# Linear attention into a four-expert mixture on one core: a sixth sum buffer, token differences in 1 KB tiles, a shared rest buffer, and batch 1's q and x rests turned by DMA

## The chip, the cores and the metric

One core of a Trainium2 chip runs the whole kernel in one launch. The metric is device time in microseconds (us), from the launch to the end of the program on that core.

## The reference, cut to what matters

```python
def phi(x): return np.where(x > 0, x, np.exp(x) - 1.0) + 1.0
q_p, k_p = phi(q), phi(k)                          # q, k, v: 8 batches, 8 heads, 576 rows, 64 columns
kv  = np.einsum('bhsd,bhse->bhde', k_p, v)
z   = np.sum(k_p, axis=2)
num = np.einsum('bhsd,bhde->bhse', q_p, kv)
den = np.einsum('bhsd,bhd->bhs', q_p, z)[..., None] + 1e-06
x   = (num / den).transpose(0, 2, 1, 3).reshape(4608, 512)
p   = domain_probs / (domain_probs.sum(-1, keepdims=True) + 1e-09)
out = sum(p[:, e:e+1] * (np.maximum(x @ w1[e], 0) @ w2[e]) for e in range(4))
```

The first half makes 4608 tokens of 512 numbers out of eight batches of 576 rows; the second half sends every token through four two-layer networks (512 to 1024 to 512) and adds their outputs, weighted.

## The kernel before

**Tiles and batches.** A batch has 576 rows: 512 of them make one tile of 512 tokens, and the last 64 are its *rest*. The eight rests together make a ninth tile. The tiles run in the order 0 to 6, then the tile of the rests (8), then 7. While TensorE runs the two layers of one tile, the attention of a later batch is made beside it: batch b's x must stand, turned (columns on partitions), before tile b begins.

**A tile's two layers.** For each expert, `Block` (L883) makes the hidden rows in two halves d with seven products each, p1 to p7, a fast scheme for a 2 by 2 block product. It needs sums of the weights (`weight_sums`, `weight_sums2`) and four differences of the tile's turned x, which `token_sum` (L870) makes, on GpSimd from tile 1 on: `tt[0]` to `tt[3]`, each 128 x 2 x 256 in float16, 1 KB a partition. p5 reads `tt[0]`, p6 `tt[1]`, p7 `tt[2]`, p4 `tt[3]`. Layer 2 (`layer2_product`, L815) works the same way with sums of the hidden rows that GpSimd makes (`hidden_sum`, L800, tiles `hs`). `add_acc` (L728) weighs a product and adds it into one of four sums `acc` per tile (128 x 512, float32, 2 KB a partition): ScalarE writes a sum's half first (L734), VectorE adds to it (L736), and `store` (L714) sends the finished sum out from SyncE's DMA queue.

**A batch's attention.** SyncE's queue loads q, k and v in four pieces each (`load`, L325). `phi_act` and `phi_dve` (L357, L374) make phi on ScalarE and VectorE, `kv` (L464) the 64 x 65 products, `dma_qT` (L417) turns q with a DMA that transposes, `nd` and `norm` (L495, L485) make x, `dma_xT` (L551) turns x. The rests go the same way in small: `load_left` (L311) loads k, v and q rest into the tile `rl`; `left_act`, `left_v` and `left_dve` (L386 to L407) make phi; `dma_qTl` (L425) turns q rest into `qz` with two transposing DMAs; `nd_left` (L514) makes x rest `x_sl` and turns it into `xT_left` with two transposing DMAs. Batch 1 is the exception: `pe_qTl` (L433) and `pe_xl` (L442) turn its two rests on TensorE, two 128 x 128 transposes each, and ScalarE copies each result out of PSUM in two pieces.

**Buffers.** A pool keeps a number of equal buffers under a tag; a new tile takes one whose last reader has gone, and its first writer waits for that reader. The tags of interest: `acc` (5 buffers of 2 KB, NACC, L173), `tt` (2 of 4 KB, one for a tile's four differences; batch 0's x lies in one of them at first), `h` (5 of 4 KB, NHB, the hidden rows and batch 0's q), `rl` of batches 1 to 7 (one buffer of 3 KB with k, v and q rest side by side).

**What sets the order.** Nothing is reordered by a planner at build time. Each engine does its instructions in the order in which the program emits them. `CFG["EARLY"]` (L103) is a hand-written list of steps that is emitted first; it reaches to the beginning of tile 2. Everything behind it is emitted by positions: `batch_steps` (L963) and the loops below L1084 give each step a place (a tile has 56 units), and the steps are sorted by it. In the names of steps, `b2.q1` is batch 2's second piece of q, `b2.next` the loads of the next batch's rests, `ts2.3` the fourth difference of tile 2, `p5.131` product 5 of tile 1, expert 3, half 1, and `m12.60` a layer 2 product of tile 1, expert 2.

Of the kernel before, what the change touches and what calls it, by code (L numbers as in the profile page):

```python
# [11 lines left out]
FP32 = mybir.dt.float32  # L12
# [123 lines left out]
    ),  # L136
# [4 lines left out]
def kernel(  # L141
# [30 lines left out]
    DE = D + 1  # L172
    NACC = 5  # L173
    NHB = 5
# [122 lines left out]
    class Batch:  # L297
# [7 lines left out]
        def alloc_left(self):  # L305
            if self.b:
                self.rl = praw.tile([P, 3, HG, D], FP32, tag="rawl", bufs=1, name="rl")
            else:
                self.rl = pm.tile([P, 2, HG, D], FP32, tag="acc", bufs=NACC, name="rl")

        def load_left(self, *names, eng=nc.sync, us=(0, 1)):  # L311
            b = self.b
            if self.rl is None:
                self.alloc_left()
            for i, (name, src) in enumerate((("k", k), ("v", v), ("q", q))):
                for u in us:
                    if name in names:
                        eng.dma_start(
                            out=self.rl[u * HP : (u + 1) * HP, i if self.b else 0],
                            in_=src[b, u * HG : (u + 1) * HG, SM:S].rearrange(  # L320
                                "h r d -> r h d"
                            ),
                        )
# [62 lines left out]
        def left_act(self, *names):  # L386

            for name in names:
                i = ("k", "v", "q").index(name)
                src = self.rl[:, i if self.b else 0].rearrange("p h d -> p (h d)")  # L390
                parts = []
                for u in range(2) if name == "k" else ():
                    us = slice(u * HP, (u + 1) * HP)
                    parts.append((us, self.kl[us, 2 * u : 2 * u + 2].rearrange("p a d -> p (a d)")))
                if name == "q":
                    self.ql = pa.tile([P, HG, D], FP16, tag="qlp", bufs=1, name="qlp")
                    parts.append((slice(0, P), self.ql.rearrange("p h d -> p (h d)")))
                for us, dst in parts:
                    nc.scalar.activation(dst, src[us], AF.Identity, bias=1.0)
                el = aps([P, HG * D], FP32, "psum_el")  # L400
                nc.scalar.activation(el, src, AF.Exp)
                self.ph["l" + name] = el, parts
# [22 lines left out]
        def dma_qTl(self):  # L425
            for u in range(2):
# [4 lines left out]
                )  # L431

        def pe_qTl(self):  # L433
            ps = aps([P, 2, P], FP16, "psum_ql")
            for a in range(2):
                nc.tensor.transpose(out=ps[:, a], in_=self.ql[:, 2 * a : 2 * a + 2], identity=identh)
            yield
            for u in range(2):
                us = slice(u * HP, (u + 1) * HP)
                nc.scalar.copy(out=self.qTl[:, :, u, us], in_=ps[:, :, us])  # L440

        def pe_xl(self):  # L442
            ps = aps([P, 2, P], FP16, "psum_xl")
            for a in range(2):
                nc.tensor.transpose(out=ps[:, a], in_=self.xl[:, a], identity=identh)
            yield
            c0 = self.b * SL
            for u in range(2):
                us = slice(u * HP, (u + 1) * HP)
                nc.scalar.copy(out=xT_left[:, 2 * u : 2 * u + 2, c0 : c0 + SL], in_=ps[:, :, us])  # L450

# [62 lines left out]
        def nd_left(self, side_by_side=False):  # L514
# [15 lines left out]
            yield  # L530
            for u in range(2) if self.b != 1 else ():
                us = slice(u * HP, (u + 1) * HP)
                c0 = self.b * SL
                nc.sync.dma_start_transpose(
                    out=xT_left[:, 2 * u : 2 * u + 2, c0 : c0 + SL],
                    in_=self.xl[us].rearrange("p a i -> p (a i)"),
                )
# [22 lines left out]
    class First(Batch):  # L560

        def open(self):
            self.qp = pm.tile([P, CM, H, D], FP16, tag="h", bufs=NHB, name="qp")
            self.qT = pa.tile([P, CM, NPAIR, P], FP16, tag="qT", bufs=1, name="qT")
            self.x = pm.tile([P, NPAIR, CM, P], FP16, tag="tt", bufs=2, name="x_sb")
            self.new_xT()
# [303 lines left out]
    def token_sum(j, i, eng=nc.gpsimd):  # L870
        x = xT_of(j)
        if j not in tts:
            tts[j] = pm.tile([P, 4, 2, NH], FP16, tag="tt", bufs=2, name="tt")
        t = tts[j]
        b11, b12 = x[:, 0:2, 0:NH], x[:, 0:2, NH:NT]
        b21, b22 = x[:, 2:4, 0:NH], x[:, 2:4, NH:NT]
        a, b = ((b12, b11), (b22, t[:, 0]), (b22, b12), (b21, t[:, 1]))[i]
        eng.tensor_tensor(out=t[:, i], in0=a, in1=b, op=AO.subtract)  # L878

# [3 lines left out]
    class Block:  # L883
# [48 lines left out]
        def p6(self):  # L932
            self.products(self.b, lambda k: s_block(self.e, 1, k), tts[self.j][:, 1])
            yield
            self.u2 = self.copy("u2", 2)

        def p5(self):
            self.products(self.e5, lambda k: s_block(self.e, 0, k), tts[self.j][:, 0], True)

        def p7(self):  # L940
            self.products(self.b, lambda k: a_block(self.e, 1, 0, k), tts[self.j][:, 2])
            yield
# [5 lines left out]
        def p4(self):  # L948
            self.products(self.b, lambda k: a_block(self.e, 1, 1, k), tts[self.j][:, 3])
            yield  # L950
# [12 lines left out]
    def batch_steps(bt, nxt, put, at, at_next):  # L963
# [36 lines left out]
        put(at["kv"], f"b{b}.kv", bt.kv)  # L1000
        put(at["lqd"] + 1, f"b{b}.next", load_left, "k", "v")
        put(at["lqd"] + 1.001, f"b{b}.nextq", load_left, "q")
        if not first:
            put(at["lqd"] + 2, f"b{b}.qTl", bt.dma_qTl)
        if first:
            put(at["qtl"], f"b{b}.qTl", bt.pe_qTl)
            for i in range(NPAIR):
# [13 lines left out]
        else:  # L1021
            put(2 * NSLOT * E + at_next["kv"] - 1e-6, f"b{b}.nl", bt.nd_left, True)
        if first:
            put(at["xl"], f"b{b}.xl", bt.pe_xl)

# [158 lines left out]
```

## Time and profile before

| | |
|---|---|
| time, median of 3 runs | 483.46 us (482.79 to 484.04) |
| time of the profiled execution | 483.89 us |
| its span, first to last instruction | 482.1 us |
| granted TensorE clock, mean | 0.999 |
| TensorE matmul busy | 476.2 us, 99% of the span |
| VectorE, ScalarE, GpSimd busy | 379.1, 329.9, 358.8 us |
| DMA | 54.06 MB, 112 GB/s mean |

The profiled execution's time is 1.8 us longer than its span: that much lies before the first and behind the last instruction. In the profile's rows, PE is TensorE, PEld its weight load, DVE VectorE, ACT ScalarE, POOL GpSimd, SP SyncE; a q behind a name (SPq) is that engine's queue, which issues DMAs and waits. A timeline row reads: start, duration, engine, line, operation, what it writes and reads, count, and in brackets the idle time before it with what ended it.

### The profile page before, as it was taken

The numbers are of one execution on the slowest core, as the hardware profiler recorded it, in microseconds if no ns is written. First come the engines' busy times: TensorE is split into PE (matmuls) and PEld (weight loads), VectorE is DVE, ScalarE is ACT, GpSimd is POOL, SyncE is SP. The second block draws the span as 40 slices with busy tenths as digits, with TensorE's granted clock in tenths as the row PEclk, the third lists the DMA queues.
The fourth block names the chain that finished last, engine by engine and source line by source line (L and its number), as shares of the span: only waits on it lengthen the run. The fifth ranks groups of instructions, "written<-read, shape, count | busy, mean of one in ns | idle before, by whom it ended". The sixth has DMA issues, their size and how long they took to land.

```text
span 482.1 us, 12029 instructions
## 1 busy us (share of the span) xinstructions
PE 476.2 (99%) x4565; PEld 406.7 (84%) x4565; DVE 379.1 (79%) x794; ACT 329.9 (68%) x659; POOL 358.8 (74%) x343
## 2 busy tenths in 40 slices
PE   9999999999999999999999999999999999999996
PEld 3776757898889888988888888988898888888886
DVE  5868998897868796888678885988787756775677
ACT  4688969956795599649884888478954465446540
POOL 5666144788966986789777977697769877987775
PEclk9999999999999999999999999999999999999999
DMA  8999997532454154624562347323320020003002
GB/s 291 218 217 262 234 224 225 141 91 82 132 158 107 31 158 148 135 57 116 171 151 51 104 130 182 68 68 113 93 44 13 1 88 1 1 2 88 2 1 87
DMA packets 80489, 54.06 MB, mean 112 GB/s; under 512 B 45536, under 2 KB 73184, under 8 KB 80432
## 3 DMA queue, kind: packets, MB, share of 16 engines
q1 hardware_dynamic: 70288, 40.89, 31.9%
q0 software_dynamic: 8896, 11.34, 12.1%
q10 hardware_dynamic: 1248, 1.08, 0.7%
q8 instruction: 35, 0.57, 0.5%
q14 instruction: 22, 0.18, 0.1%
HBM read 45.16 MB, written 9.44 MB: 113 GB/s over the span
## 4 chain that ended last, share of the span: by engine, by line
PE 93%; DMA 2%; POOL 2%; DVE 1%; ACT 1%; issue 1%; SPq 0%; POOLq 0%
PE py L840 38%; PE pb L897 25%; PE pe L897 19%; PE py L745 6%; PE ph L685 1%; PE psum_nd L500 1%; DMA rawq<-in_q_dram 1%; DMA xT<-x_sb 1%; PE psum_kv L472 1%; PE pb L840 1%; POOL tt L878 1%; PE pe L840 1%; POOL hs L813 0%; POOL hs L807 0%; PE psum_nl L519 0%
## 5 line engine op out<-in xcount | busy, mean ns | idle before, releaser
L736 DVE SCALAR_TENSOR_TENSOR acc<-py,p_sb,acc 128x256 f32<-128x256 f32 (+1 forms) x382 | 182.2, 488 | 44.4 <-PE py L840 39.8
L881 DVE CUSTOM_DVE_ANT_0 h<-pe,u 128x512 f16<-128x512 f32 x140 | 96.1, 688 | 43.1 <-PE pe L897 26.1
L897 PEld LDWEIGHTS <-w 128*128 128x128 f16 x1120 | 108.7, 98 | 16.3
L807 POOL TENSOR_TENSOR hs<-h 128x512 f16<-128x512 f16 x64 | 73.8, 1154 | 55.6 <-DVE h L881 54.2
L840 PEld LDWEIGHTS <-h 128*128 128x128 f16 x1024 | 99.7, 98 | 11.6
L840 PE MATMUL py<-w,h 128*128 128x256 f16 x744 | 106.6, 273 | 0.0
L908 ACT COPY u<-pb 128x512 f32<-128x512 f32 x140 | 82.7, 593 | 31.0 <-PE pb L897 28.7
L809 POOL TENSOR_TENSOR hs<-hs,h 128x512 f16<-128x512 f16 x64 | 74.2, 1160 | 24.3 <-PE py L840 21.8
L897 PEld LDWEIGHTS <-s 128*128 128x128 f16 x840 | 81.2, 98 | 11.8
L897 PE MATMUL pb<-tt,w 128*128 128x256 f16 x560 | 83.9, 273 | 0.0
L840 PEld LDWEIGHTS <-hs 128*128 128x128 f16 x768 | 74.2, 98 | 9.2 <-POOL hs L807 0.3
L813 POOL TENSOR_TENSOR hs<-h,hs 128x512 f16<-128x512 f16 x64 | 74.8, 1168 | 1.2 <-POOL h L811 0.6
L840 PE MATMUL py<-t,hs 128*128 128x256 f16 x496 | 74.3, 273 | 0.1
L811 POOL TENSOR_TENSOR h<-h 128x512 f16<-128x512 f16 x64 | 74.3, 1161 | 0.1
L930 ACT ACTIVATE h<-pe 128x512 f16<-128x512 f32 x70 | 42.1, 601 | 41.7 <-PE pe L897 41.2
L923 ACT COPY pe<-pb 128x512 f32<-128x512 f32 x70 | 40.1, 574 | 40.1 <-PE pb L897 14.8
L951 ACT ACTIVATE h<-pb 128x512 f16<-128x512 f32 x70 | 41.9, 600 | 5.4 <-PE pb L897 5.4
L897 PE MATMUL pb<-tt,s 128*128 128x256 f16 x280 | 41.9, 273 | 0.0
L897 PE MATMUL pe<-tt,s 128*128 128x256 f16 x280 | 41.9, 273 | 0.0
L897 PE MATMUL pe<-xT,s 128*128 128x256 f16 x248 | 37.1, 273 | 0.0
L897 PE MATMUL pe<-xT,w 128*128 128x256 f16 x248 | 37.1, 273 | 0.0
L897 PE MATMUL pb<-xT,w 128*128 128x256 f16 x248 | 36.9, 273 | 0.0
(134 smaller groups left out, 596.9 us busy)
## 6 DMA issues: line engine op xcount, KB each, us to landing
w<-in_moe_w_dram POOLq DMA_DIRECT2D x14, 512.0 KB, 10.3
out_dram<-acc SPq DMA_DIRECT2D x28, 256.0 KB, 2.5
rawb<-in_k_dram SPq DMA_DIRECT2D x24, 256.0 KB, 3.2
rawb<-in_q_dram SPq DMA_DIRECT2D x24, 256.0 KB, 2.7
rawb<-in_v_dram SPq DMA_DIRECT2D x24, 256.0 KB, 3.0
out_dram<-acc SPq DMA_DIRECT2D x12, 128.0 KB, 2.3
w<-in_moe_w_dram POOLq DMA_DIRECT2D x4, 256.0 KB, 5.5
rawb<-in_k_dram POOLq DMA_DIRECT2D x4, 256.0 KB, 10.4
```

The costliest lines, as they stand in the source:

```text
L736: nc.vector.scalar_tensor_tensor(out=acc, in0=ps, scalar=pscal, in1=acc, op0=AO.mult, op1=AO.add)
L807: nc.gpsimd.tensor_tensor(out=hs[0], in0=a21, in1=a22, op=AO.add)
L809: nc.gpsimd.tensor_tensor(out=hs[1], in0=hs[0], in1=a11, op=AO.subtract)
L811: nc.gpsimd.tensor_tensor(out=a21, in0=a11, in1=a21, op=AO.subtract)
L813: nc.gpsimd.tensor_tensor(out=hs[3], in0=a12, in1=hs[1], op=AO.subtract)
L840: nc.tensor.matmul(out=ps, lhsT=lhsT(k), rhs=rhs[:, k], start=first and k == 0, stop=k == FH - 1, skip_group_check=True,)
L881: nc.vector._custom_dve(TENSOR_ADD_SAT, out=out, in0=ps, in1=u, s0=BIG, s1=0.0)
L897: nc.tensor.matmul(out=ps[:, kk], lhsT=lk(kc), rhs=rhs[:, kc], start=first and kk == 0 and kc == 0, stop=kc == 1, skip_group_check=True,)
L908: nc.scalar.copy(u, self.b)
L923: nc.scalar.copy(self.e5, self.b)
L930: nc.scalar.activation(self.h[:, :, 0, 0:NH], self.e5, AF.Relu)
L951: nc.scalar.activation(self.h[:, :, 1, 0:NH], self.b, AF.Relu)
```

## The change

Six edits, in the order of the file:

1. `acc` has six buffers in place of five (NACC).
2. `rl` has two places in place of three: q rest is loaded to the place where k rest stood (`i % 2`).
3. `pe_qTl` and `pe_xl` go; batch 1's q rest and x rest are turned by the same transposing DMAs as the other batches' (two each, on SyncE's queue).
4. Batch 0's x takes a buffer of `h` in place of one of `tt`.
5. Each of a tile's four differences is a tile of its own: `tt` has seven buffers of 1 KB in place of two of 4 KB.
6. The order: q rest of batches 2 to 7 is loaded one position ahead of that batch's kv (step `loadlq`), behind its k rest's reading, in place of together with k and v rest; `next` is split into `nextk` and `nextv`. In the hand-written list `b1.nextv` stands behind `b1.load5` (where `b1.nextq` stood), `b2.loadlq` behind `b2.load11`, `b1.qTl` once in place of twice, and `b1.xl` is gone.

The partition's memory is the same before and after: `rl` gives 1 KB and `tt` 1 KB, and the sixth `acc` takes 2 KB.

```diff
-        "p2.031 ... b1.nd31 b1.xT3 b1.next",
-        "b2.load2 b2.load1 b1.load4 b1.load3 b1.load2 ... y2.22 b1.load5 b1.nextq b2.load0 y2.03 b1.lqm",
+        "p2.031 ... b1.nd31 b1.xT3 b1.nextk",
+        "b2.load2 b2.load1 b1.load4 b1.load3 b1.load2 ... y2.22 b1.load5 b1.nextv b2.load0 y2.03 b1.lqm",
...
-    NACC = 5
+    NACC = 6
...
-                self.rl = praw.tile([P, 3, HG, D], FP32, tag="rawl", bufs=1, name="rl")
+                self.rl = praw.tile([P, 2, HG, D], FP32, tag="rawl", bufs=1, name="rl")
...
-                            out=self.rl[u * HP : (u + 1) * HP, i if self.b else 0],
+                            out=self.rl[u * HP : (u + 1) * HP, i % 2],
...
-        def pe_qTl(self):
...
-        def pe_xl(self):
...
-            for u in range(2) if self.b != 1 else ():
+            for u in range(2):
                 us = slice(u * HP, (u + 1) * HP)
                 c0 = self.b * SL
                 nc.sync.dma_start_transpose(
...
-            self.x = pm.tile([P, NPAIR, CM, P], FP16, tag="tt", bufs=2, name="x_sb")
+            self.x = pm.tile([P, NPAIR, CM, P], FP16, tag="h", bufs=NHB, name="x_sb")
...
-        if j not in tts:
-            tts[j] = pm.tile([P, 4, 2, NH], FP16, tag="tt", bufs=2, name="tt")
-        t = tts[j]
+        t = tts.setdefault(j, [None] * 4)
+        t[i] = pm.tile([P, 2, NH], FP16, tag="tt", bufs=7, name="tt")
...
-        put(at["lqd"] + 1, f"b{b}.next", load_left, "k", "v")
-        put(at["lqd"] + 1.001, f"b{b}.nextq", load_left, "q")
         if not first:
-            put(at["lqd"] + 2, f"b{b}.qTl", bt.dma_qTl)
+            put(at["kv"] - 1, f"b{b}.loadlq", bt.load_left, "q")
+        for n in "kv":
+            put(at["lqd"] + 1, f"b{b}.next{n}", load_left, n)
+        put(at["qtl"] if first else at["lqd"] + 2, f"b{b}.qTl", bt.dma_qTl)
         if first:
-            put(at["qtl"], f"b{b}.qTl", bt.pe_qTl)
...
-        if first:
-            put(at["xl"], f"b{b}.xl", bt.pe_xl)
```

In the built programs, the rows of TensorE's order differ by the four transposes that go, ScalarE's by four copies, GpSimd's and VectorE's not at all; SyncE's queue holds four more transposing DMAs, and the q rest loads stand in other places.

More of the change, by code (lines that the diff above doesn't have):

```diff
@@ L389, in left_act @@
                 i = ("k", "v", "q").index(name)
-                src = self.rl[:, i if self.b else 0].rearrange("p h d -> p (h d)")
+                src = self.rl[:, i % 2].rearrange("p h d -> p (h d)")
                 parts = []
@@ L431, in dma_qTl @@
                 )
-        def pe_qTl(self):
[L434 to L440, printed above, removed]
-        def pe_xl(self):
[L443 to L450, printed above, removed]
         def pe_qT(self, pair, eng=nc.vector):
@@ L871, in token_sum @@
         x = xT_of(j)
-        if j not in tts:
-            tts[j] = pm.tile([P, 4, 2, NH], FP16, tag="tt", bufs=2, name="tt")
-        t = tts[j]
+        t = tts.setdefault(j, [None] * 4)
+        t[i] = pm.tile([P, 2, NH], FP16, tag="tt", bufs=7, name="tt")
         b11, b12 = x[:, 0:2, 0:NH], x[:, 0:2, NH:NT]
         b21, b22 = x[:, 2:4, 0:NH], x[:, 2:4, NH:NT]
-        a, b = ((b12, b11), (b22, t[:, 0]), (b22, b12), (b21, t[:, 1]))[i]
-        eng.tensor_tensor(out=t[:, i], in0=a, in1=b, op=AO.subtract)
+        a, b = ((b12, b11), (b22, t[0]), (b22, b12), (b21, t[1]))[i]
+        eng.tensor_tensor(out=t[i], in0=a, in1=b, op=AO.subtract)
     def add_relu(out, ps, u):
@@ L932, in p6 @@
         def p6(self):
-            self.products(self.b, lambda k: s_block(self.e, 1, k), tts[self.j][:, 1])
+            self.products(self.b, lambda k: s_block(self.e, 1, k), tts[self.j][1])
             yield
@@ L937, in p5 @@
         def p5(self):
-            self.products(self.e5, lambda k: s_block(self.e, 0, k), tts[self.j][:, 0], True)
+            self.products(self.e5, lambda k: s_block(self.e, 0, k), tts[self.j][0], True)
         def p7(self):
-            self.products(self.b, lambda k: a_block(self.e, 1, 0, k), tts[self.j][:, 2])
+            self.products(self.b, lambda k: a_block(self.e, 1, 0, k), tts[self.j][2])
             yield
@@ L948, in p4 @@
         def p4(self):
-            self.products(self.b, lambda k: a_block(self.e, 1, 1, k), tts[self.j][:, 3])
+            self.products(self.b, lambda k: a_block(self.e, 1, 1, k), tts[self.j][3])
             yield
```

16 rows, old and new, of the table nl are left out of this document.

## The prediction

> **What bounds the kernel now.** I read the page's busy times first, then the table of stretches, then the waits of TensorE, and last the timelines of the places that the change touches. The page:
>
> ```profile
> PE 476.2 (99%) x4565; PEld 406.7 (84%) x4565; DVE 379.1 (79%) x794; ACT 329.9 (68%) x659; POOL 358.8 (74%) x343
> ```
>
> One row of the table of stretches (window, its length, then busy us of PE, PEld, DVE, ACT, POOL, the granted clock, the DMA share and GB/s) and all that TensorE's weight loads waited for from 20 us on (total, times, longest; for the matmuls themselves the view has no row there):
>
> ```profile
> 140.00:470.00 330.00, 330.00 (x3206) 294.99 (x3205) 255.16 (x543) 219.99 (x433) 264.74 (x239) 1.00 0.31 79
> ```
>
> ```profile
> PEld L519 <- issue: 1.1, 5, 0.2
> PEld L472 <- issue: 0.4, 2, 0.2
> PEld L840 <- POOL hs L807: 0.3, 1, 0.3
> PEld L840 <- issue: 0.2, 1, 0.2
> ```
>
> TensorE has no idle time in 330 us at the full clock, and from 20 us on its weight loads lose 2.0 us in all, of which 1.7 is "issue": nothing was waited for. Only one wait of 0.3 us has another engine behind it. So a buffer that comes free earlier, or a transfer that lands earlier, can give back 0.3 us at most; beyond that the time falls only by what TensorE no longer executes. The first 20 us and the tail behind the last matmul hold no instruction that the change takes away or moves. Every engine beside TensorE may lose time only as far as its work still lies beneath TensorE's.
>
> **The change, part by part.**
>
> *The four transposes that go.* A batch's pair on TensorE, what ScalarE copies out of it, and the second pair:
>
> ```profile
> 78.43 0.28 PE L436 MATMUL psum_ql<-identh,qlp 128*128 128x128 f16 x2
> 78.54 0.59 PE L745 MATMUL py<-w,h 128*128 128x512 f16 x2
> ```
>
> ```profile
> L440 ACT COPY qz<-psum_ql x2: 289/294/299, 79.7 to 79.9; 128x128 f16<-128x128 f16 x2
> ```
>
> ```profile
> L445 PE MATMUL psum_xl<-identh,x_sl x2: 219/220/220, 111.5 to 111.6; 128*128 128x128 f16 x2
> ```
>
> The 0.28 is a pipelined duration; what counts is that the next group starts 78.54 - 78.43 = 0.11 us later. Two pairs: 2 x 0.11 = **-0.22 us** on TensorE, which is the path. ScalarE loses 2 x 2 copies of about 0.29, some 1.2 us, off the path: worth nothing by themselves. The Trainium skill (TensorE: Matmul & The Clock Gate, Part 4: PE-mode transpose) gives about 275 ns for such a transpose inside a kernel; by that figure the four would be worth an estimated 1.1 us and the result 482.1. The spacing of 0.11 us for two in this trace says otherwise, and I go by it.
>
> *The transfers in their place.* SyncE's queue now issues four more transposing DMAs, two for q rest behind the second store of the row 79.81 and two for x rest behind the load of 114.44. The q rest loads (two each) move behind a batch's last k loads: batch 2's to behind the row 81.78, batch 3's from the row 104.23 to behind 126.75, and so on for each batch. Batch 2's v rest goes out where its q rest did before. What one costs the queue, and the queue itself:
>
> ```profile
> L428 SPq DMA_TRANSPOSE qz<-qlp x14: 1159/1187/2296, 95.9 to 342.2; - x14
> ```
>
> ```profile
> L318 SPq DMA_DIRECT2D rl<-in_q_dram x16: 607/616/1650, 45.9 to 301.4; - x16
> ```
>
> ```profile
> 79.81 1.92 SPq L717 DMA_DIRECT2D out_dram<-acc  x2
> 81.78 1.01 SPq L340 DMA_DIRECT2D rawb<-in_k_dram  x2
> 84.30 0.37 SPq L340 DMA_DIRECT2D rawb<-in_v_dram  x1
> 84.76 0.42 SPq L717 DMA_DIRECT2D out_dram<-acc  x1
> 90.19 2.65 SPq L420 DMA_TRANSPOSE qT<-qp  x2
> ...
> 104.23 1.27 SPq L318 DMA_DIRECT2D rl<-in_q_dram  x2
> 105.60 2.55 SPq L554 DMA_TRANSPOSE xT<-x_sb  x2
> 108.25 0.53 SPq L340 DMA_DIRECT2D rawb<-in_v_dram  x1
> 108.89 1.19 SPq L554 DMA_TRANSPOSE xT<-x_sb  x1
> 114.44 0.37 SPq L340 DMA_DIRECT2D rawb<-in_k_dram  x1
> 117.27 8.82 SPq L340 DMA_DIRECT2D rawb<-in_q_dram  x4
> 126.75 1.68 SPq L340 DMA_DIRECT2D rawb<-in_k_dram  x2
> 130.93 1.23 SPq L717 DMA_DIRECT2D out_dram<-acc  x2
> ```
>
> First place, 80 to 90: two transposes (2 x 1.19) and two q rest loads (2 x 0.62) put 3.6 us more into the queue. It is done at 84.76 + 0.42 = 85.2 and then stands idle until q is ready at 90.19, that is 5.0 us. The loads and stores between slip by up to 3.6 us, and the qT turn behind them by nothing: cost 0. Second place: 114.44 + 0.37 = 114.81 to 117.27 are 2.5 us free, two transposes take 2.4: cost 0. Third: 126.75 + 1.68 = 128.43 to 130.93 are 2.5 us free, 1.2 are needed: cost 0; the same place comes once per batch. Bounds: nothing below (no one waits for these transfers sooner than for TensorE's copies of before), and above what the issue takes at its longest, 2 x 2.30 + 2 x 1.65 = 7.9 us in the first place, 2.9 more than the idle time there. I take 0, the medians being 3.6.
>
> *Where the queue gets shorter.* The same q rest loads leave the row 104.23, ahead of batch 2's turns of x. GpSimd waits for the last of these:
>
> ```profile
> 111.69 1.15 POOL L809 TENSOR_TENSOR hs<-hs,h 128x512 f16<-128x512 f16 x1
> 113.82 0.24 POOL L352 MEMSET vp<- 128x32 f16 x1 [0.98 <-DMA xT<-x_sb]
> ...
> 123.11 1.15 POOL L807 TENSOR_TENSOR hs<-h 128x512 f16<-128x512 f16 x1
> ```
>
> ```profile
> 107.99 0.29 DVE L488 TENSOR_TENSOR x_sb<-psum_nd,recip 128x128 f16<-128x128 f32 x1
> ```
>
> GpSimd is idle for 0.98 us until 113.82, then works without a gap to 123.11 + 1.15 = 124.26, and that last sum is what TensorE's 0.3 us wait ends on. The last xT was issued at 108.89 because the queue was full until 108.25 + 0.53; its data stood at 107.99 + 0.29 = 108.28. Without the two loads the queue runs 1.27 us ahead, so the last xT goes at about 108.4, bound by its data: 0.5 us earlier, and as the v load of 108.25 then goes 1.4 us ahead of it rather than 0.6, it may also land faster. GpSimd is then 0.5 to 0.98 us earlier, at least the 0.3 us of the wait plus the 0.11 by which TensorE itself comes sooner. Behind the stall TensorE's queue has no other wait. Worth **-0.3 us**.
>
> *Six sums.* What the engines that write `acc` waited for (the answer for this tile):
>
> ```profile
> its engine sat idle before it (us, times) until:
>   PE py L840: 42.9, 116
>   issue: 0.6, 2
>   ACT h L951: 0.3, 1
>   PE py L745: 0.2, 1
> ```
>
> No store is among them: a writer of a sum never idled for a buffer. The sixth buffer gives 0, and it covers the stores that now leave up to 3.6 us later at 80 to 85.
>
> *Seven differences of 1 KB.* While one tile's four are in use, three buffers are free, so the next tile's last difference has to take the one of `tt[1]`, read last by p6 of expert 3. That adds a wait on GpSimd, with the next batch's memset and hidden sums queued behind it. The fourth difference of tile 3, and that product of tile 2:
>
> ```profile
> 166.69 1.16 POOL L878 TENSOR_TENSOR tt<-xT,tt 128x512 f16<-128x512 f16 x1
> ```
>
> ```profile
> 163.11 0.60 PE L897 MATMUL pb<-tt,s 128*128 128x256 f16 x4
> ```
>
> The reader is done at 163.71, 3.0 us ahead of the writer: cost 0, and 3.0 us of cover. Batch 0's x in `h`:
>
> ```profile
> L674 ACT COPY xT<-psum_xh x6: 372/373/377, 15.0 to 22.1; 128x256 f16<-128x256 f16 x6
> ```
>
> ```profile
> L930 ACT ACTIVATE h<-pe x70: 591/598/688, 26.3 to 463.5; 128x512 f16<-128x512 f32 x70
> ```
>
> Its last turned piece is copied at 22.1, and a hidden half of expert 1, the first that could take its buffer, is written from 26.3 on: cost 0, with 4 us of cover. The other added waits have old answers: q rest into k rest's place, and the writers of q rest and x rest behind the new transposes, each have most of a batch's stage between reader and writer.
>
> *The sum.* -0.22 - 0.3 = -0.5 us. Against the profiled execution, 483.89 - 0.5 = 483.4; it lies 0.43 above the median of the runs, 483.46, against which the forecast is **483.0 us**.
>
> **Rivals.**
>
> *The stall stays.* If GpSimd is not earlier (the last xT waits on other traffic: it took until 113.8, 4.9 us after its issue), the 0.3 us stays and the second pair's 0.11 turns into a longer wait: -0.11 alone, 483.3. For it: the transfer's landing is the least known number here. Against it: its issue is bound by data that do not move.
>
> *The queue overflows before 90.19 (slower).* If the four new DMAs take more than the 5.0 us that are free there, the qT turn goes late, and with it batch 2's numerators, its xT and GpSimd's chain to 124.26; each us over 5.0 (less the 0.5 gained at 108.89) becomes a stall of TensorE. At the longest issues seen, 7.9 us, that is 2.9 - 0.5 = 2.4 us on top of -0.22: 485.6. For it: the q rest loads go out while stores and loads are landing, and one such load did take 1.65 us to issue. Against it: medians of 1.19 and 0.62.
>
> *A bubble that buffers cure (faster).* The seven "issue" gaps at L519 and L472 come once per batch, 1.5 us in all. If missing buffers caused them, six sums would end them: 483.0 - 1.5 = 481.5. Against it: the rows name no releaser, and these lines write PSUM and read none of the changed tiles. The Trainium skill (Perfetto Trace Analysis, Optimization Strategy) says of a gap that repeats on the engine that should be saturated that it can mean too little memory for the next tile; the row "issue" does not agree.
>
> *The change doesn't do what it says:* the sixth sum is without effect by the rows above, and the forecast counts it so.
>
> **Chances.** Forecast 0.61, stall stays 0.22, overflow 0.13, bubble 0.03, 0.01 for the rest (slower). About 0.3%, 1.45 us, is what a measurement of this kernel can tell from no change. The first two are within it; the overflow at 2.4 us is beyond it, the bubble on the other side: faster 0.03, same 0.83, slower 0.14. The range: below, the lowest run lies 0.7 under the median, so 482.3; above, from 483.3 into the overflow as far as half of its 2.4 us, rounded up: 485.0.
>
> **What the next profile would show.** Right: no L436 and L445, PE busy about 0.2 lower; SyncE's first xT of the 105.60 row at about 104.3 and the last at 108.4; POOL's memset idle below 0.5 us; no PEld wait on POOL hs; qT still at about 90; no DMA in the idle list of `acc`; the same seven "issue" gaps. Wrong: an idle row of PE or PEld with ACT, DVE or POOL behind it, above all between 80 and 130 us; a qT turn later than 90.5; POOL idle ahead of a `tt` row on PE.

## The result, and the profile after

| | before | after |
|---|---|---|
| time, median (14 runs each, same chip) | 483.69 us (482.79 to 484.40) | **483.03 us** (482.40 to 483.43) |
| ratio | | 0.9981, 95% interval 0.9974 to 0.9988 |
| time of the profiled execution, its span | 483.89, 482.1 us | 483.27, 481.5 us |

The changed kernel is faster by 0.12 to 0.26%, some 0.9 us by the ratio (the two medians lie 0.66 us apart): inside what the prediction called no change, and close to its 483.0. A second set of 11 runs (below) gave 0.9977. Two things do not fit the prediction's sum of -0.5, though: the gain is about twice that, and the slowest run of after lies below the median of before. The rest of this document is about that difference.

First the steps that the prediction named. The page of after, and all that TensorE's weight loads waited for from 20 us on:

```profile
PE 475.9 (99%) x4561; PEld 407.3 (85%) x4561; DVE 379.6 (79%) x794; ACT 329.2 (68%) x655; POOL 358.7 (75%) x343
```

```profile
PEld L500 <- issue: 1.1, 5, 0.2
PEld L453 <- issue: 0.4, 2, 0.2
PEld L821 <- issue: 0.2, 1, 0.2
```

Four matmuls less, 0.3 us less of busy PE, the seven "issue" gaps as before (L519 and L472 are now L500 and L453), and no row with POOL behind it. SyncE's queue of after (timeline; SPq rows are issues):

```profile
80.31 2.52 SPq L428 DMA_TRANSPOSE qz<-qlp  x2
...
84.53 2.44 SPq L318 DMA_DIRECT2D rl<-in_q_dram  x2
87.07 0.55 SPq L340 DMA_DIRECT2D rawb<-in_v_dram  x1
87.72 0.41 SPq L698 DMA_DIRECT2D out_dram<-acc  x1
90.05 2.65 SPq L420 DMA_TRANSPOSE qT<-qp  x2
...
104.66 2.54 SPq L535 DMA_TRANSPOSE xT<-x_sb  x2
107.30 0.54 SPq L340 DMA_DIRECT2D rawb<-in_v_dram  x1
108.18 1.19 SPq L535 DMA_TRANSPOSE xT<-x_sb  x1
113.17 0.37 SPq L340 DMA_DIRECT2D rawb<-in_k_dram  x1
113.60 2.44 SPq L515 DMA_TRANSPOSE xT_left<-x_sl  x2
117.02 8.83 SPq L340 DMA_DIRECT2D rawb<-in_q_dram  x4
```

The first place took 2.52 + 2.44 = 5.0 us in place of the 3.6 of the medians; it was done at 88.13, 1.9 us ahead of the qT turn, which went at 90.05. The first xT went at 104.66 (forecast 104.3), the last at 108.18 (108.4), and the x rest turns fit ahead of 117. GpSimd's memset and the hidden sum behind it:

```profile
112.28 0.24 POOL L352 MEMSET vp<- 128x32 f16 x1
...
121.57 1.16 POOL L788 TENSOR_TENSOR hs<-h 128x512 f16<-128x512 f16 x1
```

No idle bracket, and 1.54 us earlier than the 113.82 and 123.11 of before. Laid against before matmul by matmul, TensorE of after gains 0.11 us at 78.5, 0.11 at 111.6 and 0.23 at 124; it loses 0.14 at 340, where a copy of ScalarE starts 0.12 us after the copy ahead of it has ended, with its input ready (L888 at 337.72; the profile names no cause):

```profile
337.02 0.57 ACT L903 COPY pe<-pb 128x512 f32<-128x512 f32 x1
337.72 0.59 ACT L888 COPY u<-pb 128x512 f32<-128x512 f32 x1
```

The last matmul is thus 0.35 us earlier, and the span 0.62: the other 0.27 come behind the last matmul.

### The profile page after: what moved, and what is told of

Its sections match the earlier page's. It is cut to its first block, busy times and chain, and to the rows that moved or that the text cites. A ratio compares the mean times of both kernels' runs of the same rounds, so it can differ in the third digit from the quotient of the medians.

```text
span 481.5 us, 12040 instructions
## 1 busy us (share of the span) xinstructions
PE 475.9 (99%) x4561; PEld 407.3 (85%) x4561; DVE 379.6 (79%) x794; ACT 329.2 (68%) x655; POOL 358.7 (75%) x343
## 4 chain that ended last, share of the span: by engine, by line
PE 96%; DVE 1%; DMA 1%; ACT 1%; issue 0%; SPq 0%
PE py L821 39%; PE pb L877 25%; PE pe L877 19%; PE py L726 6%; PE ph L666 1%; PE psum_nd L481 1%; DMA rawq<-in_q_dram 1%; PE psum_kv L453 1%; PE pb L821 1%; PE pe L821 1%; PE psum_nl L500 0%; DVE kpos L577 0%; ACT ee L592 0%; PE psum_num L639 0%; PE warm_ps L1008 0%; PE psum_xh L653 0%
## 5 line engine op out<-in xcount | busy, mean ns | idle before, releaser
L888 ACT COPY u<-pb 128x512 f32<-128x512 f32 x140 | 82.7, 593 | 31.3 <-PE pb L877 28.8
```

The lines of the kernel that those rows point to most:

```text
L888: nc.scalar.copy(u, self.b)
```

## The experiments

The theory at the start is the prediction's: the transposes and GpSimd's stall carry the gain, the sums and the other buffers none. The first four kernels ask which part carries what. They led to a rival, **W** (a writer of a sum waits for a store), which the next ones test, and to **T** for the 0.27 us behind the last matmul (the tail). Ratios are to the kernel before, in runs on the same chip.

### The parts one by one

The changed kernel with five sums:

```diff
-    NACC = 6
+    NACC = 5
```

> The changed kernel with five sum buffers again, nothing else undone. Theory A (two pairs of transposes less on TensorE, 0.22 us, and a shorter SyncE queue ahead of batch 2's turns of x, 0.23 us; the sums and the difference tiles give nothing): the last matmul starts where it does in the changed kernel, 477.8 us, give or take 0.15; time 483.0; TensorE waits for no other engine between 20 and 300 us. The store that now goes out at 82.9 instead of 81.4 lands at about 87.4, and the writer of the sum that takes its buffer comes at 87.8: a margin of 0.4 us, so a stall of up to 0.2 us near 88 is possible. Theory B (the sixth sum is what gives): the last matmul starts at 478.1 or later, time 483.5 or more, and the idle list of the sums names a store.

Before, with nothing but the turns by DMA:

```diff
-            for u in range(2) if self.b != 1 else ():
+            for u in range(2):
...
-            put(at["qtl"], f"b{b}.qTl", bt.pe_qTl)
+            put(at["qtl"], f"b{b}.qTl", bt.dma_qTl)
...
-            put(at["xl"], f"b{b}.xl", bt.pe_xl)
```

> The kernel before with one part of the change: batch 1's two rests are turned by DMA; rest buffer, order of the rests' loads, sums and difference tiles as before. Theory A: TensorE comes 0.11 us earlier from 78.5 us and 0.22 us from 111.6; the last turn of batch 2's x is still issued at about 108.8 behind the six loads of rests, GpSimd's chain comes only 0.11 us earlier, and the wait of 0.23 us at 124 grows to about 0.34, so that 0.11 us is left at the last matmul (478.06); time 483.6 against 483.7 of the kernel before. Theory B: the same as before within 0.05 us at the last matmul.

Before, with q rest in k rest's place and the loads' new order alone:

```diff
-                self.rl = praw.tile([P, 3, HG, D], FP32, tag="rawl", bufs=1, name="rl")
+                self.rl = praw.tile([P, 2, HG, D], FP32, tag="rawl", bufs=1, name="rl")
...
-        put(at["lqd"] + 1.001, f"b{b}.nextq", load_left, "q")
...
+            put(at["kv"] - 1, f"b{b}.loadlq", bt.load_left, "q")
```

> The kernel before with one part of the change: k and q rest share a place and q rest is loaded later; the four transposes stay on TensorE, sums and difference tiles as before. Theory A: nothing until 124 us, where the wait for GpSimd's hidden sum goes, 0.23 us; the last turn of batch 2's x is issued at about 108.4 and GpSimd's idle time at 113.8 falls from 0.98 to under 0.5; last matmul at 477.94; time 483.45. Theory B: 0.05 us or less.

Before, with the seven small differences and x in `h` alone:

```diff
-            self.x = pm.tile([P, NPAIR, CM, P], FP16, tag="tt", bufs=2, name="x_sb")
+            self.x = pm.tile([P, NPAIR, CM, P], FP16, tag="h", bufs=NHB, name="x_sb")
...
-            tts[j] = pm.tile([P, 4, 2, NH], FP16, tag="tt", bufs=2, name="tt")
...
+        t[i] = pm.tile([P, 2, NH], FP16, tag="tt", bufs=7, name="tt")
```

> The kernel before with one part of the change: seven difference tiles of 1 KB and batch 0's x in a buffer of the hidden rows; all else as before. Theory A: no change beyond 0.05 us at the last matmul (478.17), the wait of 0.23 us at 124 stays; time 483.7. Theory B (finer tiles come free earlier): GpSimd starts a difference earlier somewhere, and the last matmul comes at least 0.1 us earlier.

Measured, before being at 483.82 us (31 runs), ten runs each: five sums 483.35, 0.9984 (0.9973 to 0.9995); turns 483.43, 0.9989 (0.9979 to 0.9999); shared rest 484.04, 0.9998 (0.9986 to 1.0011); differences 483.58, 0.9991 (0.9981 to 1.0001). The times alone separate little.

The place of the last matmul, which the expectations name, does not decide either, because the beginning differs from execution to execution: laid against before's first profile, TensorE stands at 20 us between 0.83 us earlier and 0.08 later in the profiles of this document, with no order by kernel. So the last matmul of five sums starts at 477.76, where theory A has it, although its profile lost 0.5 us to waits of the kind of theory B: its beginning was 0.44 us shorter. What is compared below is therefore what TensorE lost at a place, not where it ended.

There the profiles do separate: all four have five sums, and all four show in ScalarE's waits a row that neither before nor after has. From five sums, then from the turns:

```profile
ACT acc L715 <- DMA out_dram<-acc: 1.0, 2, 0.6
```

```profile
ACT acc L734 <- DMA out_dram<-acc: 1.3, 2, 0.9
```

So the first write of a sum does wait for a store. TensorE stands still for a part of it, as in the timeline of the turns:

```profile
291.33 0.60 PE L897 MATMUL pb<-xT,w 128*128 128x256 f16 x4
292.29 0.60 PE L840 MATMUL py<-w,h 128*128 128x256 f16 x4 [0.36 <-ACT acc L734]
```

This is theory **W**: with five sums ScalarE's first write into a sum waits for a landing, in many executions though not in the one of before that was profiled, and the sixth buffer ends that. The reason can be read from the code: a tile has four sums, and with five buffers its fourth sum takes the buffer of the tile before's *third*; with six, that of its *second*, which went out 3.7 us earlier (284.42 against 288.13). The profile of before has the wait just met. Its third store of that tile went out at 288.13 (timeline), landed 2.9 us after its issue (DMA view of this one issue), and ScalarE's copy ahead of the write ended at 291.02 + 0.61 = 291.63 (consecutive rows of ScalarE overlap a little):

```profile
288.13 0.81 SPq L717 DMA_DIRECT2D out_dram<-acc  x2
```

```profile
out_dram<-acc SPq DMA_DIRECT2D x1, 256.0 KB, 2.9
```

```profile
291.02 0.61 ACT L908 COPY u<-pb 128x512 f32<-128x512 f32 x1
291.48 0.52 ACT L734 ACTIVATE acc<-py,p_sb 128x256 f32<-128x256 f32 x1
```

Landed at 291.03, needed at 291.63: 0.6 us to spare. At 138, 190 and 241 it was 0.9, 0.7 and 0.25. The stores of this profile landed in 1.8 to 4.7 us, so the next execution may miss.

### The same kernels again

No edit: before, after, and after with five sums, for second profiles; and six sums with all the rest, but batch 1's rests turned on TensorE as in before.

> The kernel before once more, unchanged, for a second profile. Theory W (with five sums ScalarE's first write into a sum can have to wait until the store of that buffer's last sum has landed; whether it does changes from execution to execution): the write follows the landing of the third tile's store by only 0.25 to 0.9 us in the first profile, at 138, 189, 240, 291, and such landings took 1.8 to 4.3 us in the profiles so far; so this profile should have one to three rows of ACT acc on DMA out_dram in ScalarE's waits, 0.3 to 1.3 us together, and a gap of TensorE of 0.1 to 0.6 us behind each at 138, 190, 241, 292 or 343. Theory of the prediction (the sums wait for nothing): none, as in the first profile. Time: 1.000 of before.

> The changed kernel once more, for a second profile. Theory W: with six sums the first writes follow the landings of their stores by 3.6 us or more (up to 390 us), so no row of ACT acc on DMA out_dram and no gap of TensorE at 138, 190, 241, 292; the time is 0.998 of before, 0.5 from instructions and GpSimd's stall, the rest from the stores. The stall of 0.14 us at 340, which its first profile shows, should come again if it belongs to the order of the instructions. Theory of the prediction: 0.999 of before (483.3 if before is at 483.8), nothing seen of the stores either.

> The changed kernel with five sums in place of six, once more. Theory W: 0.3 to 0.5 us slower than the changed kernel in the same call, and in its profile one to four rows of ACT acc on DMA out_dram, with a gap of TensorE behind each. Theory of the prediction: the same time as the changed kernel within 0.2 us, no such row.

```diff
-            for u in range(2):
+            for u in range(2) if self.b != 1 else ():
...
+            put(at["qtl"], f"b{b}.qTl", bt.pe_qTl)
...
+            put(at["xl"], f"b{b}.xl", bt.pe_xl)
```

> Six sums, the small differences, q rest in k rest's place and the loads' new order, but batch 1's q rest and x rest turned by TensorE as before. Theory W: 0.22 us more than the changed kernel and 0.3 to 0.5 less than the five sums of the same call or so: 483.25 where the changed kernel is at 483.0 and before at 483.7; no row of ACT acc on DMA out_dram. Theory of the prediction: 0.22 us more than the changed kernel, and no less than the kernel with five sums.

Measured, before being at 484.19 us (33 runs), eleven runs each:

| | median | lowest to highest | ratio |
|---|---|---|---|
| before again | 484.29 | 483.62 to 484.59 | 1.0003 (0.9994 to 1.0012) |
| after again | **482.85** | 482.77 to 483.33 | **0.9977** (0.9968 to 0.9986) |
| after, five sums | 483.77 | 482.78 to 484.42 | 0.9992 (0.9983 to 1.0001) |
| six sums, no turns by DMA | 483.52 | 483.17 to 483.84 | 0.9987 (0.9978 to 0.9996) |

The sixth buffer alone is worth 483.77 - 482.85 = 0.9 us by the medians here and 0.0015 x 484.19 = 0.7 by the ratios, where 0.3 to 0.5 were expected; from the first sets' ratios it is 0.0003 x 483.7 = 0.15 us. The intervals are wide, some 0.5 us either way. The runs also agree better: here they spread over 0.56 us with six and over 1.64 with five, whose fastest run is as fast as the six's; in the first sets it was 1.03 and 2.02. A wait that comes in some executions looks so, though the differences of the beginning add to both.

Before's second profile had the stall that the first one lacked, 0.33 us of TensorE at 292. Five sums had two. The expected rows of ACT acc on DMA out_dram stand in neither list, as both profiles put the same wait down to another engine. The second stall of five sums, in the timelines of SyncE, ScalarE and TensorE, with the landing of the store of 237.43:

```profile
237.43 0.82 SPq L698 DMA_DIRECT2D out_dram<-acc  x2
238.34 0.40 SPq L340 DMA_DIRECT2D rawb<-in_v_dram  x1
238.84 1.95 SPq L340 DMA_DIRECT2D rawb<-in_k_dram  x1
```

```profile
out_dram<-acc SPq DMA_DIRECT2D x1, 256.0 KB, 4.5
```

```profile
242.01 0.47 ACT L715 ACTIVATE acc<-py,p_sb 128x256 f32<-128x256 f32 x1 [1.09 <-PE pb L877]
```

```profile
241.40 0.60 PE L877 MATMUL pb<-xT,w 128*128 128x256 f16 x4
242.54 0.60 PE L821 MATMUL py<-w,h 128*128 128x256 f16 x4 [0.53 <-ACT acc L715]
```

Issued at 237.43, landed at 241.91, written at 242.01. Two reading lessons are in these rows. The bracket of ScalarE names PE's `pb`, which the write does not read; its own product had ended at 240.7 by the trace. The wait had several releasers, and the row names the one whose signal came last; only the landing tells. And not all of ScalarE's delay is TensorE's: in the thirteen stalls between 138 and 297 us, over all these profiles and that of the late stores below, TensorE lost the time by which the landing missed the need, less 0.3 us. (In two more, at 343, it lost that time and 0.1 more.)

In the Trainium skill (DMA: Bandwidth & Descriptors, Anatomy of one DMA) a transfer that GpSimd issues takes a fixed 2.0 us plus its bytes at 436 GB/s, by which 256 KB would land in an estimated 2.6 us. These stores go out from SyncE, so the rule is only a near one; their median of 2.4 in this profile is close to it, the 4.5 is not, and the late landing is what stalls. Late landings go with a load close behind the store. Over twelve profiles (all but those of the ten turns and of the late stores below), 21 third stores between 134 and 289 us had the next load of v at least 1.4 us behind them and landed within 3.3 us; 27 had it some 0.9 us behind, and 19 of these took 3.7 to 4.5. The load is not the whole of it: the other 8, before's of 288.13 among them, landed in 2.9 to 3.3, and at 339, where no such load follows, four of twelve took 3.7 to 4.4. What else delays a landing stays open.

What TensorE lost at these places, beyond the usual spacing of its matmuls, in every profile with five sums: before 0 and 0.33, five sums 0.52 and 1.25, turns 0.52, shared rest 0, differences 1.05, and 0.88 in the kernel with four loads below; **0.57 on average**. In all five profiles of six sums: 0. (Shared rest lost 0.30 us at another place, 70.6, where ScalarE idled 0.99 us for a load of k; no other profile with the new load order has that.) GpSimd's stall at 124 is of the same kind: with the load order of before it is 0.23, 0, 0.21, 0 and 0 in five profiles (before twice, turns, differences, four loads), 0.09 on average, and 0 in every one with the new order.

The kernel without the turns was to be 0.22 us above after and is 0.67 above by the medians, 0.5 by the ratios: 0.27 of the difference is the next subject, the 0.14 at 340, which it lacks, work the other way, and the rest lies within the intervals.

### Behind the last matmul

From the end of the last matmul to the end of the span are 3.6 us in before, both times, in shared rest, differences and six sums without turns; 3.4 in after, both times, in five sums, both times, and in turns. The four kernels with 3.6 are those with TensorE's turns. When SyncE's waits at the end begin, in us after the last matmul's end (from the trace):

```
before 0.49 1.11 1.66 2.28 2.51 2.57 2.63 2.69 2.75  end 3.6
after  0.49 0.55 0.61 0.68 0.79 1.15 1.70 2.16 2.48  end 3.4
```

In the program the DMAs report to eight counters in turn, and at the end SyncE asks one counter after the other, in fixed order, some 0.06 us each. In before the last two stores have the third and fourth counter, and four that are full by then are asked behind them: 4 x 0.06 = 0.24 us. The change adds four DMAs, which shifts the turn by four, and the last store is asked last. If so, four DMAs of any kind should do it.

```diff
+            if len(stores) == 28:
+                for n in range(4):
+                    eng.dma_start(out=few[:, n], in_=k[0, 0, 0:P, 2 * n : 2 * n + 2])
```

> The kernel before, and four loads of 1 KB into a tile of their own that nothing reads, on SyncE at about 389 us, where its queue is empty. Theory T (the tail: the eight completion counters of the DMAs go round in turn, and at the end SyncE waits for them one after the other in fixed order, some 0.06 us each; in before the last two stores' counters stand in the middle, and four that were done long ago are still asked behind them; four more DMAs turn the order by four, and the last store's counter is asked last): the time from the last matmul to the end of the span falls from 3.9 to 3.65 us, and the ratio is 0.9995. Rival (the 0.27 us between the tails of the two kernels is chance): the tail stays at 3.9, ratio 1.0000.

> The changed kernel with the same four loads of 1 KB at about 389 us. Theory T: the order turns back to that of before, the tail grows from 3.65 to 3.9 us, and the ratio to before rises by 0.0005 to about 0.9985. Rival: the tail stays at 3.65, the ratio at 0.998.

(These two count the tail from the *start* of the last matmul, 0.27 us earlier.) The tail is 3.4 us in before with the loads, and 3.6 in after with them: T holds, both ways. The two kernels below agree: eight DMAs more than after, a whole turn of the counters, leave the tail at 3.4, and twenty more, two turns and a half, make it 3.7. With the order of after, asks lie beside the flight of the stores, and SyncE waits less for these. Its waits for stores at the end, in before, after, before with four loads, after with four loads:

```profile
SPq L1179 <- DMA out_dram<-acc: 1.9, 4, 0.6
```

```profile
SPq L1157 <- DMA out_dram<-acc: 1.5, 4, 0.5
```

```profile
SPq L1186 <- DMA out_dram<-acc: 1.5, 4, 0.5
```

```profile
SPq L1164 <- DMA out_dram<-acc: 1.8, 4, 0.7
```

The times lean the same way and cannot show so little alone: 0.9998 (0.9989 to 1.0008) for before with the loads, 0.9985 (0.9977 to 0.9994) for after with them, before being at 483.80.

### The rival's price: a queue that overflows

The changed kernel with eight more turns in the first place:

```diff
-            for u in range(2):
+            for u in (0, 1) * (5 if self.b == 1 else 1):
```

> The changed kernel, and behind batch 1's two turns of q rest eight more of the same (the same data to the same place; 8 x 1.19 = 9.5 us of SyncE's queue). The changed kernel's queue is idle there only from 88.1 to 90.05, 1.9 us, so batch 2's qT turn should go 7.6 us late, at about 97.7. The rival of the prediction (each us beyond the idle time becomes a stall of TensorE, less 0.5): 7.1 to 7.6 us longer. With TensorE's own cover added (in the profile of before the numerators read qT 2.2 us after its last piece has landed): 5.4 us longer. If SyncE's queue has no part in the time: nothing.

Measured: 491.49 us, 1.0157 (1.0143 to 1.0171), some 8.5 us more than after. Timeline of SyncE and a row of its waits, timeline of TensorE, and the table of stretches (PE, PEld, DVE, ACT, POOL, granted clock, DMA share, GB/s):

```profile
79.51 15.14 SPq L428 DMA_TRANSPOSE qz<-qlp  x10
...
99.33 2.92 SPq L420 DMA_TRANSPOSE qT<-qp  x2
```

```profile
SPq L428 <- DMA qz<-qlp: 1.6, 1, 1.6
```

```profile
94.53 0.23 PE L500 MATMUL psum_nl<-kvz,qz 128*128 128x130 f16 x1 [4.37 <-DMA qz<-qlp]
95.80 0.51 PE L500 MATMUL psum_nl<-kvz,qz 128*128 128x130 f16 x3 [1.04 <-DMA qz<-qlp]
...
104.01 0.34 PE L481 MATMUL psum_nd<-kvz,qT 128*128 128x130 f16 x3 [1.61 <-DMA qT<-qp]
```

```profile
95.00:99.00 4.00, 3.20 (x19) 2.45 (x20) 0.05 (x1) 1.70 (x4) 1.16 (x1) 0.57 0.70 214
```

The queue's part was real, but the path was not the one expected. The ten turns took 15.14 us, not ten times 1.19, because the third waited 1.6 us for the landing of the first, into whose place it writes (the row of SyncE's waits), and was 2.0 us in issue; the other nine took 1.19 to 1.23 each. So qT went 9.3 us late. The first to wait was the reader of q rest itself, as the extra turns write the tile that it reads (a flaw of this kernel): 5.7 us between 89.9 and 96. Then TensorE ran at half clock for 3.4 us, which cost 1.4, and then came 1.8 for qT. The first qT landed at 103.96, 4.6 us after its issue, where after has 90.05 + 3.2 = 93.3; TensorE read it 8.4 us later than after does, so the cover that was expected was there, 2.3 us by these rows, and 1.4 of it went to the slower landing. The 8.5 us fit the rival's price of about one us of time per us of overflow, but they do not show it alone: only 1.8 of them are a wait for qT, which came when the other waits had already used up the rest. In after the queue has 1.9 us to spare there, and no such wait.

### The store later

The changed kernel with five sums, and four loads of 1 KB ahead of the third store of tiles 1 to 5:

```diff
+        if 0 < j < 6 and ns == 2:
+            for n in range(4):
+                eng.dma_start(out=few[:, n], in_=k[0, 0, 0:P, 2 * n : 2 * n + 2])
```

> The changed kernel with five sums, and four loads of 1 KB (0.48 us of SyncE each) into a tile that nothing reads ahead of the third store of tiles 1 to 5. SyncE is idle for some 0.7 us ahead of that store, so it goes 1.2 us later. Theory W: the first write into the same buffer, by the next tile's fourth sum, waits 1.2 us longer; in the profiles so far TensorE lost the write's delay less 0.3, so the gaps at 138, 190, 241 and 292 become 0.5 to 1.3 us each, 3.5 in all, where five sums had 0.6 on average: about 3 us slower than with five sums, ratio to before about 1.005, and ScalarE's waits show acc on DMA out_dram. Theory of the prediction (no writer of a sum waits for a store): the time of five sums, ratio 0.999. If it is rather the loads behind the store that come late, the gaps stand elsewhere and have another releaser.

Measured: 490.48 us, 1.0154 (1.0122 to 1.0186): about 7 us slower than with five sums, twice what was expected. The third stores left 1.5 to 2.9 us later behind the second ones than in before, not 1.2: the four loads took 2.7 us of the queue in the first place and 3.4 in the second, and 2.0 in the other three. The place is the expected one. All that TensorE's matmuls waited for from 20 us on, what ScalarE waited for, and one of the five:

```profile
PE py L826 <- ACT acc L720: 5.8, 5, 1.5
```

```profile
ACT acc L720 <- DMA out_dram<-acc: 6.3, 4, 2.1
```

```profile
192.03 0.47 ACT L720 ACTIVATE acc<-py,p_sb 128x256 f32<-128x256 f32 x1 [2.10 <-DMA out_dram<-acc]
```

One stall in each of five tiles, 0.9 to 1.7 us against the usual spacing, 6.7 us in all, and no stall elsewhere; the profiled execution took 489.80 us, which without them is 483.1. The landing of the third store is what limits the kernel with five sums.

## Why the prediction was right, and where it was not

The time and the verdict came out, the sum behind them did not. It was -0.5 and what was found is about -1.0; that the forecast of 483.0 stood so near was luck: it was laid against 483.46, a median of three runs, and more runs of before gave 483.69, 483.82 and 484.19.

- **The transposes, -0.22:** right in place and size, twice 0.11. The 275 ns for each that the Trainium skill gives (TensorE: Matmul & The Clock Gate, Part 4: PE-mode transpose), an estimated 1.1 us for the four, were not seen.
- **GpSimd's stall, -0.3:** right in mechanism: the xT issues earlier, GpSimd's idle gone, the wait gone. Too large as a term: it was 0.23 us in before's profile, and it stood in two of five with that load order, 0.09 on average. "The stall stays" did not come.
- **"Six sums ... 0": this is the step that failed.** The row "a writer of a sum never idled for a buffer" was true of one execution. It does not say by how much the writer missed the wait, and that was 0.25 to 0.9 us on a landing that scatters by more than two. The bound that the prediction drew from the same profile, that a buffer that comes free earlier can give back 0.3 us at most, fails with it. The term is about -0.57, a mean of eight profiles from 0 to 1.25, and the largest of all. "A bubble that buffers cure" looked for it at the seven "issue" gaps, which stayed; and the rival by which the sixth sum is without effect, counted into the forecast, is refuted.
- **The seven differences, x in `h`, q rest in k rest's place: 0.** No stall in the profiles is put down to them, but for the one of 0.30 us at 70 in shared rest, behind a load of k. With the differences alone the ratio was 0.9991, its interval just reaching 1.0001.
- **The turns in SyncE's queue: 0.** Right in every place, with 1.9 us to spare in the first where the medians gave 1.4 (5.0 - 3.6). Not foreseen: four more DMAs turn the order of the counters at the end, **-0.27**. The prediction left the tail out because no instruction of it moves; that is so, and yet what SyncE waits for there changes.
- **The stall of 0.14 us at 340**, not foreseen, is in three of the four profiles of six sums with turns by DMA and in none of the others: +0.14. Its cause stays open.

The new sum: -0.22 - 0.09 - 0.57 - 0.27 + 0.14 = -1.0 us, against -0.9 and -1.1 from the two ratios (0.0019 x 483.69, 0.0023 x 484.19). For six sums without the turns it gives -0.66, measured 0.0013 x 484.19 = -0.63; for the turns alone -0.49, measured -0.53; for after with five sums -0.58, measured -0.77 and -0.39. For before with four loads it gives -0.27, measured -0.10, inside its interval; for after with them -0.74, measured -0.73; for shared rest alone -0.09, measured -0.10; for the differences alone 0, measured -0.44, at the edge of its interval. Each measured value is known to about 0.5 us either way, so sums that come out to a tenth are partly luck, and the terms rest on the profiles.

## What to carry to other kernels

A view of waits shows only the waits that were lost, and only in that execution. For every buffer that a DMA frees, work out from the rows how long before its next writer the landing came, and set that against the spread of landings (minimum to maximum) of such transfers: where the margin is smaller than the spread, another buffer is worth something even though the profile shows no wait. Runs of one kernel that spread by 0.3 to 0.4% while another's agree within 0.1 to 0.2% can be a sign of such a wait; only a second and third profile show whether it is.

## What the runs showed of the hardware that was not expected

- **The end of a program** costs SyncE about 0.06 us for each completion counter that it still asks behind the last store's; the number of DMAs, eight counters in turn, decides how many that are: 3.4 or 3.6 us for the same stores.
- **Half clock after a pause.** In the kernel with ten turns TensorE stood 4.5 us and, after one matmul, 1.2 more; its matmuls of 256 columns were then spaced 0.214 us in place of 0.109, and by the trace the clock was halved for 3.4 us, from 95.2 on; the row of 95 to 99 us has a granted clock of 0.57. The Trainium skill (TensorE: Matmul & The Clock Gate, Part 1: The HAM clock gate) has the clock halved after an idle window of about 3.4 us and full again after a busy one of that length; the trace agrees. The stalls of up to 1.7 us in the profile of the kernel with late stores left the clock at 1.00.
- **Small DMAs** are not small for the queue: 1 KB a load took 0.43 us to issue at the median, up to 1.84, while a load of 256 KB took 0.37 at the median of before and after.
